# Pooled attention and a gated two-layer block in one kernel: batch 1's k pooled on GpSimd, its v on VectorE, and four accumulators for the first down product

## The chip, the core and the metric

The kernel runs on one core of a Trainium2 chip. The core has TensorE (matrix products, written to PSUM), VectorE, ScalarE (activation functions), GpSimd and SyncE, each with an instruction queue of its own that runs in order, and 16 DMA engines that move data between HBM and SBUF. Engines wait for each other and for transfers by semaphores. The metric is the device time of one execution in microseconds (us).

Names in the profile: PE is TensorE's matmul, PEld its weight load, DVE is VectorE, ACT ScalarE, POOL GpSimd, SP SyncE. `L321` is line 321 of the kernel before. A program's tile names stand without their numbers: `bank` for bank0 to bank2.

## The reference

```python
def _attn_ref(q, k, v) -> np.ndarray:
    B, H, S, D = q.shape
    pool = 8
    Sp = S // pool
    scale = 1.0 / np.sqrt(D)
    k_p = k.reshape(B, H, Sp, pool, D).mean(axis=3)
    v_p = v.reshape(B, H, Sp, pool, D).mean(axis=3)
    scores = scale * np.matmul(q, k_p.transpose(0, 1, 3, 2))
    scores = scores - np.max(scores, axis=-1, keepdims=True)
    attn = np.exp(scores)
    attn = attn / (np.sum(attn, axis=-1, keepdims=True) + 1e-09)
    return np.matmul(attn, v_p).astype(np.float32)

def _moe_ref(x, w_in, w_out) -> np.ndarray:
    h = x @ w_in
    g = h * np.cos(h)
    return (g @ w_out).astype(np.float32)
```

q, k and v are 8 x 8 x 576 x 64 (batch, heads, rows, width), so Sp is 72; `w_in` is 512 x 2048 and `w_out` 2048 x 512. The attention's output, with its heads side by side, is x: 8 batches of 576 rows are 4608 tokens of width 512.

## The kernel before

**Tiles.** The 4608 tokens are worked in nine tiles of 512 (`NT`, loop variable `t`). Batches have 576 rows, so a tile's attention comes from two batches: while tile `t` is worked, the last 64 rows of batch `t` (`REST`) and the first 512 rows of batch `t+1` (variable `b`) go through the attention. The instructions of each engine run in the order in which the program emits them.

**A tile's two phases.** The up phase has eight steps `fp` of eight matmuls each (`up_mm`, L321): x transposed (`xT`) times `w_in`, into `banks[fp % 3]`. There are three `banks`, each a pair of PSUM banks, and two single `obanks`. `up_g` takes the cosine on ScalarE (L328) and multiplies on VectorE (L331) into `g_sb`. For tiles after the first, the first half of steps 0 and 1 is emitted ahead of the rest. The down phase has 64 matmuls (`down_mm`, L334): for each of four groups of 128 tokens (`ms`) 16 chunks of the inner dimension (`fc`), accumulated in `obanks[ms % 2]`, then copied out by VectorE and stored by SyncE (`down_out`, L340, L344).

**Fillers.** The list `fill` of pairs (n, function) puts the attention's TensorE work between the down matmuls: a function is emitted ahead of down matmul n. `scores` (L214, with the exponential on ScalarE at L221) and `values` (L244: matmuls, then logarithm and exponential on ScalarE, L250 and L251, then two multiplies on VectorE into `xT`, L255) work a unit of 256 rows by four heads, or `REST` by all eight heads. Both write one of `banks`, and it is free for the next user when the exponential, or for values the last multiply, has read it. Units of batch 1 are `us[0]` to `us[3]`: heads 0 to 3 and then 4 to 7, two blocks of rows each.

**Batches 0 and 1 before, and the others.** The loads of q, k and v go through GpSimd's DMA queue, which converts fp32 to bf16; the weights go through it as well. For batches 0 and 1 k and v are laid out over 128 rows (`load_even`) and pooled on TensorE with a matrix of ones (`groups`): `pool_k_mm`, 72 matmuls (L160), and `pool_v_mm`, 18 (L168), with copies out of PSUM by `put_kk` (L132) and L170. For batch 1, k's pooling is emitted at step 4 of tile 0's up phase, the 18 transposes of q (L195, copies L196) at steps 5 and 6, and v's pooling ahead of down matmul 8. From batch 2 on k and v are loaded with eight rows side by side over 72 partitions (`load_kv`, L103) and pooled on GpSimd by three rounds of adds (`pool_add`, L142, L145, then L148 for k, written twice, or L151 for v); k is transposed by a DMA on SyncE (`k_transpose`), q by another.

**Loads around the change.** The order on GpSimd's queue is: q, k, q, v of batch 0; `w_in` blocks 0 to 2; k of batch 1; half of its q; `w_in` block 3; the other half; `w_out` block 0; v of batch 1; three memsets; `w_out` blocks 1 to 3; and, emitted after tile 0, k, q and v of batch 2 and the pooling of batch 2 (the second part of v's in tile 1). The staging tiles `kv_st` have two buffers, handed out in turn: in before one holds k and v of batch 0 and the other those of batch 1, then each one k or one v.

**Tile 0's down matmuls** go in an order of their own, since the last `w_out` blocks arrive late: for each half of the tokens (two `ms`) through the four `w_out` blocks, so block c is first used by matmul 8c, and each half's two accumulators are the two `obanks`.

Of the kernel before, what the change touches and what calls it, by code (L numbers as in the profile page):

```python
# [14 lines left out]
POOL = 8  # L15
# [4 lines left out]
def kernel(  # L20
# [65 lines left out]
    def kv_tile():  # L86
        return kvst.tile([128, 2 * H * POOL * D], BF16, name="kv_st", tag="kv_st")
# [11 lines left out]

    def load_kv(b, which, src):  # L100

        st = kv_tile()[:Sp].rearrange("p (i h t d) -> p i h t d", i=2, h=H, t=POOL)
        nc.gpsimd.dma_start(out=st[:, 0].rearrange("p h t d -> p h (t d)"),  # L103
                            in_=src[b].rearrange("h (p t) d -> p h (t d)", t=POOL))
        staged[which, b] = st

# [26 lines left out]

    def pool_add(b, which, part=None):

        st = staged[which, b]
        x = st[:, 0]
        s = st[:, 1].rearrange("p h t d -> p (h t d)").bitcast(FP32).rearrange(
            "p (h t d) -> p h t d", h=H, t=POOL // 2)
        add = nc.gpsimd.tensor_tensor  # L140
        if part != 1:
            add(out=s, in0=x[:, :, 0:4, :], in1=x[:, :, 4:8, :], op=ADD)  # L142
        if part == 0:
            return
        add(out=s[:, :, 0:2, :], in0=s[:, :, 0:2, :], in1=s[:, :, 2:4, :], op=ADD)  # L145
        if which == "k":
            for slot in range(2):
                add(out=kp2[b % 2][:Sp, :, slot, :], in0=s[:, :, 0, :], in1=s[:, :, 1, :], op=ADD)  # L148
        else:
            s = s.rearrange("p (j a) t d -> p j a t d", a=2)  # L150
            add(out=v_part(b), in0=s[..., 0, :], in1=s[..., 1, :], op=ADD)  # L151

# [20 lines left out]
    def k_transpose(b):  # L173
        nc.sync.dma_start_transpose(out=kk[b % 2], in_=kp2[b % 2].rearrange("p h s d -> p (h s d)"))


    QB = KCH * ROW // 2
# [218 lines left out]

    kv_even_tiles(1)
    q_tile(1)
    for cg in range(3):
        load_w_in(cg)  # L400
    load_even(staged["k", 1], 1, k)
    load_even(staged["q", 1], 1, q, 0, 2)
    load_w_in(3)
    load_even(staged["q", 1], 1, q, 2, 4)
    load_w_out(0)
    load_even(staged["v", 1], 1, v)
    nc.gpsimd.memset(vz[1], float(POOL))
    for i in range(2):
        nc.gpsimd.memset(kp2[i], 0.0)
    for cg in range(1, 4):  # L410
        load_w_out(cg)

# [43 lines left out]
    for t in range(NT):  # L456
# [5 lines left out]
        for fp in range(FFCH // 2):  # L462
            up_mm(t, fp, 2 if fp < 2 else 0)
            between = ()
            if t == 0:
                if fp == 4:
                    puts = pool_k_mm(1, obanks[0], 0, 2), pool_k_mm(1, obanks[1], 2, 4)
                elif fp in (5, 6):
                    g0 = 9 * (fp - 5)
                    puts = q_transpose_mm(1, obanks[0], g0, g0 + 5), q_transpose_mm(1, obanks[1], g0 + 5, g0 + 9)  # L470
                if fp in (4, 5, 6):
                    puts[0](vec)
                    between = ((puts[1], act),)
            up_g(t, fp, between)
            if 0 < t and b < B:
                if fp == 0:
                    q_transpose(b)
                elif fp == 2:
                    k_transpose(b)
                    if t == 1:  # L480
                        load_next(b)
                        pool_add(b, "v", 1)
                        load_kv(b + 1, "v", v)
        mms = [(ms, fc) for ms in range(4) for fc in range(FFCH)]
        if t == 0:
            mms = [(ms, fc) for hm in range(2) for cg in range(4) for ms in range(2 * hm, 2 * hm + 2)
                   for fc in range(4 * cg, 4 * cg + 4)]


        def S_(n, bank):  # L490
            return lambda: scores(b, us[n], banks[bank])

        later = []

        def V_(n, bank, wait=None):
            return lambda: values(b, us[n], banks[bank], wait)

# [4 lines left out]
        if t == 0:  # L502
            fill[1:] = [(2, S_(0, 0)), (8, lambda: pool_v_mm(1, banks[1])), (8, lambda: values(t, REST, banks[2])),
                        (11, S_(1, 0)), (13, V_(0, 1)), (18, S_(2, 2)), (21, V_(1, 0, later)), (26, S_(3, 1)),
                        (32, lambda: later.pop()()), (32, V_(2, 2)), (40, V_(3, 0))]
        elif b < B:
            us = BY_TOKENS

            def scores_of(*parts):

                def go():
                    for f in scores_mm, scores_exp:
                        for b_, u, bank in parts:
                            f(b_, u, banks[bank])
                return go

            def rows_of(i, blk, bank):
# [4 lines left out]
                    (42, rows_of(1, 0, 0)), (44, rows_of(1, 1, 1)), (47, lambda: values(t, REST, banks[2]))]  # L522
        fi = 0
        if t == NT - 1:
            mms = mms[:-FFCH]
        for n, (ms, fc) in enumerate(mms):
            while fi < len(fill) and fill[fi][0] <= n:
                fill[fi][1]()
                fi += 1
            down_mm(obanks[ms % 2], ms, fc)  # L530
            if fc == FFCH - 1:
                down_out(t, ms, obanks[ms % 2])
        if t < B:
# [36 lines left out]
```

## Time and profile before

| | |
|---|---|
| median of 3 runs | 297.28 us (296.84 to 297.56) |
| the profiled execution's own time | 296.36 us |
| its span, first to last instruction | 294.6 us |
| tile 0: first up matmul, first down matmul | 17.2 us, 33.6 us |
| first up matmul of tiles 1, 2 and 3 | 52.96, 83.32, 113.67 us |

The span is what the profile's rows cover; the execution's own time has 1.8 us more around it. The profile's table of busy times says how much of the span each engine worked, the slices say when, and the chain that ended last says which work the end waited for, step by step backwards.

Between 10 and 47 us the DMA engines move 206 GB/s on average. What lands when, from the DMA issues one by one (issue plus time to landing):

| load | issued, us | landed, us |
|---|---|---|
| w_in block 2 | 6.64 | 20.94 |
| k of batch 1 | 7.37 | 23.77 |
| first half of q of batch 1 | 8.10 | 25.2 |
| w_in block 3 | 9.32 | 27.8 |
| w_out block 0 | 13.56 | 31.7 |
| v of batch 1 | 16.10 | 34.5 |
| w_out blocks 1, 2, 3 | 19.51, 21.20, 24.03 | 37.1, 39.9, 42.3 |
| k, q, v of batch 2 | 25.83, 28.07, 37.52 | 46.2, 48.9, 54.2 |

### The profile page before, as it was taken

How to read it: one execution, taken by the hardware profiler on the slowest of the kernel's cores; microseconds unless marked ns; L12 is line 12 of the kernel's file. 1: busy time of each engine (PE TensorE's matmuls, PEld its weight loads, DVE VectorE, ACT ScalarE, POOL GpSimd, SP SyncE). 2: the span in 40 equal slices, each digit the busy share in tenths (PEclk: the TensorE clock that was granted, in tenths of full speed). 3: DMA queues.
4: the chain of work that ended last, by engine and by line, in shares of the span. 5: the costliest groups of instructions: out<-in, count | busy, mean ns of one | idle time of the engine just before them, and what ended most of it. 6: DMA issues, size and time to landing. Idle time of an engine off the chain costs nothing.

```text
span 294.6 us, 4775 instructions
## 1 busy us (share of the span) xinstructions
PE 287.7 (98%) x1912; PEld 140.2 (48%) x1912; DVE 158.8 (54%) x212; ACT 162.1 (55%) x182; POOL 130.5 (44%) x93
## 2 busy tenths in 40 slices
PE   8899999999999999999999999999999999999995
PEld 3545544444544454445444544455445544444444
DVE  5458647466347643764375456645574557416612
ACT  3886898365446734673468337743675456506500
POOL 8563017968973696349833983399000000000000
PEclk9999999999999999999999999999999999999999
DMA  7999999659966975698469747994603320131033
GB/s 151 204 207 206 207 205 207 137 95 178 157 155 93 167 128 131 112 170 149 108 122 169 147 92 139 162 148 103 142 2 71 81 64 0 36 73 36 0 71 73
DMA packets 57222, 36.07 MB, mean 122 GB/s; under 512 B 35185, under 2 KB 52465, under 8 KB 57201
## 3 DMA queue, kind: packets, MB, share of 16 engines
q0 software_dynamic: 19744, 18.07, 39.4%
q1 hardware_dynamic: 37216, 17.57, 28.6%
q8 instruction: 15, 0.25, 0.4%
q10 hardware_dynamic: 240, 0.13, 0.2%
q14 instruction: 7, 0.05, 0.0%
HBM read 36.70 MB, written 9.44 MB: 157 GB/s over the span
## 4 chain that ended last, share of the span: by engine, by line
PE 93%; DVE 1%; issue 0%; DVEq 0%
PE bank L321 42%; PE obank L334 42%; PE bank L214 3%; PE bank L301 2%; PE bank L244 1%; PE bank L352 1%; PE obank L160 0%; PE bank L168 0%; PE obank L283 0%; PE obank L195 0%; DVE xT L285 0%; DVE vz L170 0%; DVE o_sb L340 0%; DVEq L285 0%
## 5 line engine op out<-in xcount | busy, mean ns | idle before, releaser
L334 PE MATMUL obank<-w_out_sb,g_sb 128*128 128x512 bf16 x560 | 131.4, 379 | 0.0
L321 PE MATMUL bank<-xT,w_in_sb 128*128 128x512 bf16 x576 | 126.6, 379 | 0.0
L328 ACT ACTIVATE cos<-bank,half_pi 128x1024 f32<-128x1024 f32 x72 | 79.3, 1114 | 70.4 <-PE bank L321 70.4
L331 DVE TENSOR_TENSOR g_sb<-bank,cos 128x1024 bf16<-128x1024 f32 x72 | 87.3, 1223 | 51.6 <-ACT cos L328 51.6
L321 PEld LDWEIGHTS <-w_in_sb 128*128 128x128 bf16 x576 | 56.1, 98 | 67.6 <-issue 1.6
L334 PEld LDWEIGHTS <-g_sb 128*128 128x128 bf16 x560 | 51.6, 98 | 56.6 <-issue 2.0
L142 POOL TENSOR_TENSOR kv_st<-kv_st 72x2048 f32<-72x2048 bf16 x12 | 48.7, 4058 | 30.4 <-DMA kv_st<-in_k_dram 30.4
L340 DVE COPY o_sb<-obank 128x512 f32<-128x512 f32 x35 | 24.2, 692 | 46.9 <-PE obank L334 46.7
L221 ACT ACTIVATE ex<-bank 72x1024 bf16<-72x1024 f32 (+1 forms) x40 | 35.0, 929 | 21.2 <-PE bank L214 21.1
L145 POOL TENSOR_TENSOR kv_st<-kv_st 72x1024 f32<-72x1024 f32 x12 | 28.2, 2348 | 0.9
L250 ACT ACTIVATE lnc<-bank 64x256 f32<-64x256 f32 (+1 forms) x24 | 10.8, 449 | 17.9 <-PE bank L244 17.7
L255 DVE TENSOR_TENSOR xT<-bank,inv 64x256 bf16<-64x256 f32 (+1 forms) x24 | 12.3, 511 | 10.8 <-ACT inv L251 10.6
L304 DVE TENSOR_TENSOR x_r<-bank,inv_r 128x512 bf16<-128x512 f32 x24 | 16.6, 691 | 0.8
L148 POOL TENSOR_TENSOR kp<-kv_st 72x512 bf16<-72x512 f32 x12 | 14.9, 1265 | 0.5
L214 PE MATMUL bank<-qT,kk 64*72 64x256 bf16 (+1 forms) x192 | 11.9, 250 | 0.4 <-DVE qT L196 0.4
L214 PEld LDWEIGHTS <-kk 64*72 64x72 bf16 x192 | 7.9, 110 | 8.7 <-issue 7.4
L309 ACT ACT_TABLE_LOAD x9 | 11.5, 1283 | 0.9 <-PEq L554 0.7
L312 ACT ACT_TABLE_LOAD x9 | 11.5, 1283 | 0.2
L301 PEld LDWEIGHTS <-ex 72*128 72x128 bf16 x192 | 8.9, 97 | 5.0
L452 POOL COPY gate<-kk 1x1 bf16<-1x1 bf16 x5 | 0.9, 180 | 22.7 <-DMA kk<-kp 22.7
L302 DVE RECIPROCAL inv_r<-bank 128x8 f32<-128x8 f32 x24 | 4.8, 202 | 10.7 <-PE bank L301 10.7
L301 PE MATMUL bank<-vz,ex 72*128 72x65 bf16 x192 | 9.8, 192 | 0.0
(59 smaller groups left out, 113.9 us busy)
## 6 DMA issues: line engine op xcount, KB each, us to landing
out_dram<-o_sb SPq DMA_DIRECT2D x70, 128.0 KB, 2.4
kv_st<-in_v_dram POOLq DMA_DIRECT2D x8, 576.0 KB, 12.9
kv_st<-in_k_dram POOLq DMA_DIRECT2D x7, 576.0 KB, 7.9
q_b<-in_q_dram POOLq DMA_DIRECT2D x6, 576.0 KB, 10.0
w_in_sb<-in_moe_w_in_dram POOLq DMA_DIRECT2D x4, 512.0 KB, 13.4
w_out_sb<-in_moe_w_out_dram POOLq DMA_DIRECT2D x4, 512.0 KB, 18.2
q_b<-in_q_dram POOLq DMA_DIRECT2D x4, 288.0 KB, 12.2
g_sb<-in_k_dram SPq DMA_DIRECT2D x1, 576.0 KB, 3.6
```

The costliest lines, as they stand in the source:

```text
L142: add(out=s, in0=x[:, :, 0:4, :], in1=x[:, :, 4:8, :], op=ADD)
L145: add(out=s[:, :, 0:2, :], in0=s[:, :, 0:2, :], in1=s[:, :, 2:4, :], op=ADD)
L148: add(out=kp2[b % 2][:Sp, :, slot, :], in0=s[:, :, 0, :], in1=s[:, :, 1, :], op=ADD)
L214: nc.tensor.matmul(pair[:Sp, bank, c:c + n].rearrange("p (g n) -> p g n", n=64), lhsT=kk[b % 2][half[r], h0 + i, 0:Sp], rhs=att["qT", b][h ...
L221: nc.scalar.activation(out=ex[:, 0:nh * n].rearrange("p (a n) -> p a n", a=2), in_=pair[:Sp, :, 0:nh * n // 2], func=ACTF.Exp, scale=scale ...
L301: nc.tensor.matmul(out[:, pj, hp * (D + 1):(hp + 1) * (D + 1)], lhsT=ex[:, c:c + 128], rhs=v1)
L304: nc.vector.tensor_mul(out=x, in0=vals, in1=inv.unsqueeze(3).to_broadcast([128, KCH, 2, D]))
L321: nc.tensor.matmul(h[:, j, :], lhsT=w_in_sb[fc // 4][:, ki, (fc % 4) * 128:(fc % 4 + 1) * 128], rhs=xT[:, ki, t * TILE:(t + 1) * TILE], st ...
L328: nc.scalar.activation(out=cos, in_=h, func=ACTF.Sin, bias=half_pi[:, :1])
L331: nc.vector.tensor_mul(out=g_sb[:, 2 * fp:2 * fp + 2, :], in0=h, in1=cos)
L334: nc.tensor.matmul(o, lhsT=g_sb[:, fc, ms * 128:(ms + 1) * 128], rhs=w_out_sb[fc // 4][:, fc % 4, :], start=(fc == 0), stop=(fc == FFCH - 1))
L340: nc.vector.tensor_copy(out=o[:, 0:n], in_=ps)
```

## The change

For batch 1 alone, k and v are loaded as for later batches, over 72 partitions. k is pooled by GpSimd's adds (8.9 us of busy time for a k in the profile before), emitted between the issues of the last two `w_out` blocks, and the pooled k is transposed by eight TensorE transposes into one `obank`, with one copy out (new function `k_transpose_mm`). v is loaded in two halves of four heads and pooled by the same three rounds of adds, on VectorE, for each half. Its staging buffer is the one that batch 0's k and v had. The loads go in this order after `w_in` block 2: k, `w_in` block 3, half of q, `w_out` block 0, the other half of q, half of v, the memsets, `w_out` block 1, the other half of v, `w_out` block 2, [pooling of k], `w_out` block 3.

In tile 0's up phase only one group of nine q transposes is left, at step 6; the other nine, the k transposes and v's adds are emitted ahead of down matmuls 5, 6 and 7. Tile 0's down matmuls go through `w_out` block by block for all four groups of tokens, so block c is first used by matmul 16c, and there are four accumulators: the two halves of `banks[2]` and the two `obanks`. The four outputs are thus finished by matmuls 51, 55, 59 and 63. The scores of batch 1 are emitted in pairs of units, and the fillers use `banks[0]` and `banks[1]` alone; the last unit of values stands ahead of down matmul 52, on `banks[0]` (before: matmul 40).

```diff
@@ -97,12 +97,12 @@
     def q_tile(b):
         staged["q", b] = qst.tile([128, KCH, ROW, D], BF16, name="q_b", tag="q_b")
 
-    def load_kv(b, which, src):
-
-        st = kv_tile()[:Sp].rearrange("p (i h t d) -> p i h t d", i=2, h=H, t=POOL)
-        nc.gpsimd.dma_start(out=st[:, 0].rearrange("p h t d -> p h (t d)"),
-                            in_=src[b].rearrange("h (p t) d -> p h (t d)", t=POOL))
-        staged[which, b] = st
+    def load_kv(b, which, src, h0=0, h1=H):
+
+        if h0 == 0:
+            staged[which, b] = kv_tile()[:Sp].rearrange("p (i h t d) -> p i h t d", i=2, h=H, t=POOL)
+        nc.gpsimd.dma_start(out=staged[which, b][:, 0, h0:h1].rearrange("p h t d -> p h (t d)"),
+                            in_=src[b, h0:h1].rearrange("h (p t) d -> p h (t d)", t=POOL))
 
     def load_q(b):
         q_tile(b)
@@ -131,13 +131,12 @@
             for r in range(2):
                 copy(out=dst[half[r], pj0:pj1, a, 0:Sp], in_=ps[half[a]])
 
-    def pool_add(b, which, part=None):
+    def pool_add(b, which, part=None, add=nc.gpsimd.tensor_tensor, h0=0, h1=H):
 
         st = staged[which, b]
-        x = st[:, 0]
+        x = st[:, 0, h0:h1]
         s = st[:, 1].rearrange("p h t d -> p (h t d)").bitcast(FP32).rearrange(
-            "p (h t d) -> p h t d", h=H, t=POOL // 2)
-        add = nc.gpsimd.tensor_tensor
+            "p (h t d) -> p h t d", h=H, t=POOL // 2)[:, h0:h1]
         if part != 1:
             add(out=s, in0=x[:, :, 0:4, :], in1=x[:, :, 4:8, :], op=ADD)
         if part == 0:
@@ -148,7 +147,7 @@
                 add(out=kp2[b % 2][:Sp, :, slot, :], in0=s[:, :, 0, :], in1=s[:, :, 1, :], op=ADD)
         else:
             s = s.rearrange("p (j a) t d -> p j a t d", a=2)
-            add(out=v_part(b), in0=s[..., 0, :], in1=s[..., 1, :], op=ADD)
+            add(out=v_part(b)[:, h0 // 2:h1 // 2], in0=s[..., 0, :], in1=s[..., 1, :], op=ADD)
 
     def pool_k_mm(b, bank, pj0, pj1):
 
@@ -173,6 +172,14 @@
     def k_transpose(b):
         nc.sync.dma_start_transpose(out=kk[b % 2], in_=kp2[b % 2].rearrange("p h s d -> p (h s d)"))
 
+
+    def k_transpose_mm(b, bank):
+
+        ps = bank.bitcast(BF16)[:, 0:H * Sp].rearrange("p (h n) -> p h n", n=Sp)
+        for h in range(H):
+            nc.tensor.matmul(ps[:, h, :], kp2[b % 2][:Sp, h].rearrange("p s d -> p (s d)"), identity[:Sp, :Sp],
+                             is_transpose=True)
+        nc.vector.tensor_copy(out=kk[b % 2][:, :, 0:Sp], in_=ps)
 
     QB = KCH * ROW // 2
 
@@ -394,21 +401,23 @@
     half_pi = consts.tile([128, 1], FP32, name="half_pi")
     nc.vector.memset(half_pi, math.pi / 2.0)
 
-    kv_even_tiles(1)
     q_tile(1)
     for cg in range(3):
         load_w_in(cg)
-    load_even(staged["k", 1], 1, k)
+    load_kv(1, "k", k)
+    load_w_in(3)
     load_even(staged["q", 1], 1, q, 0, 2)
-    load_w_in(3)
+    load_w_out(0)
     load_even(staged["q", 1], 1, q, 2, 4)
-    load_w_out(0)
-    load_even(staged["v", 1], 1, v)
-    nc.gpsimd.memset(vz[1], float(POOL))
+    load_kv(1, "v", v, 0, 4)
     for i in range(2):
         nc.gpsimd.memset(kp2[i], 0.0)
-    for cg in range(1, 4):
-        load_w_out(cg)
+    nc.gpsimd.memset(vz[1], float(POOL))
+    load_w_out(1)
+    load_kv(1, "v", v, 4, 8)
+    load_w_out(2)
+    pool_add(1, "k")
+    load_w_out(3)
 
     def warm_up(n, bank):
 
@@ -463,12 +472,8 @@
             up_mm(t, fp, 2 if fp < 2 else 0)
             between = ()
             if t == 0:
-                if fp == 4:
-                    puts = pool_k_mm(1, obanks[0], 0, 2), pool_k_mm(1, obanks[1], 2, 4)
-                elif fp in (5, 6):
-                    g0 = 9 * (fp - 5)
-                    puts = q_transpose_mm(1, obanks[0], g0, g0 + 5), q_transpose_mm(1, obanks[1], g0 + 5, g0 + 9)
-                if fp in (4, 5, 6):
+                if fp == 6:
+                    puts = q_transpose_mm(1, obanks[0], 0, 5), q_transpose_mm(1, obanks[1], 5, 9)
                     puts[0](vec)
                     between = ((puts[1], act),)
             up_g(t, fp, between)
@@ -483,36 +488,39 @@
                         load_kv(b + 1, "v", v)
         mms = [(ms, fc) for ms in range(4) for fc in range(FFCH)]
         if t == 0:
-            mms = [(ms, fc) for hm in range(2) for cg in range(4) for ms in range(2 * hm, 2 * hm + 2)
-                   for fc in range(4 * cg, 4 * cg + 4)]
-
-
-        def S_(n, bank):
-            return lambda: scores(b, us[n], banks[bank])
-
-        later = []
-
-        def V_(n, bank, wait=None):
-            return lambda: values(b, us[n], banks[bank], wait)
+            mms = [(ms, fc) for cg in range(4) for ms in range(4) for fc in range(4 * cg, 4 * cg + 4)]
+
+
+        def scores_of(*parts):
+
+            def go():
+                for f in scores_mm, scores_exp:
+                    for b_, u, bank in parts:
+                        f(b_, u, banks[bank])
+            return go
+
+        def late_q():
+            puts = q_transpose_mm(1, banks[0][:, 0, :], 9, 14), q_transpose_mm(1, banks[0][:, 1, :], 14, 18)
+            puts[0](vec)
+            puts[1](act)
+
+        def pool_v():
+            for h0 in (0, 4):
+                pool_add(1, "v", add=nc.vector.tensor_tensor, h0=h0, h1=h0 + 4)
+
+        def V_(n, bank):
+            return lambda: values(b, us[n], banks[bank])
 
         fill = []
         if t < B:
             exp_tables()
             fill = [(1, lambda: scores(t, REST, banks[2])), (16, lambda: values(t, REST, banks[1]))]
         if t == 0:
-            fill[1:] = [(2, S_(0, 0)), (8, lambda: pool_v_mm(1, banks[1])), (8, lambda: values(t, REST, banks[2])),
-                        (11, S_(1, 0)), (13, V_(0, 1)), (18, S_(2, 2)), (21, V_(1, 0, later)), (26, S_(3, 1)),
-                        (32, lambda: later.pop()()), (32, V_(2, 2)), (40, V_(3, 0))]
+            fill = [(5, late_q), (6, lambda: k_transpose_mm(1, obanks[1])), (7, pool_v), (14, scores_of((1, us[0], 0), (1, us[1], 1))),
+                    (20, lambda: scores(0, REST, banks[0])), (25, scores_of((1, us[2], 0), (1, us[3], 1))),
+                    (30, V_(0, 0)), (35, V_(1, 1)), (41, lambda: values(0, REST, banks[0])), (46, V_(2, 1)), (52, V_(3, 0))]
         elif b < B:
             us = BY_TOKENS
-
-            def scores_of(*parts):
-
-                def go():
-                    for f in scores_mm, scores_exp:
-                        for b_, u, bank in parts:
-                            f(b_, u, banks[bank])
-                return go
 
             def rows_of(i, blk, bank):
                 return lambda: values_rows(b, us[2 * i:2 * i + 2], blk, banks[bank])
@@ -521,15 +529,18 @@
                     (29, scores_of((b, us[2], 0), (b, us[3], 1), (t, REST, 2))),
                     (42, rows_of(1, 0, 0)), (44, rows_of(1, 1, 1)), (47, lambda: values(t, REST, banks[2]))]
         fi = 0
+        acc = [obanks[ms % 2] for ms in range(4)]
+        if t == 0:
+            acc = [banks[2][:, 0, :], banks[2][:, 1, :], obanks[0], obanks[1]]
         if t == NT - 1:
             mms = mms[:-FFCH]
         for n, (ms, fc) in enumerate(mms):
             while fi < len(fill) and fill[fi][0] <= n:
                 fill[fi][1]()
                 fi += 1
-            down_mm(obanks[ms % 2], ms, fc)
+            down_mm(acc[ms], ms, fc)
             if fc == FFCH - 1:
-                down_out(t, ms, obanks[ms % 2])
+                down_out(t, ms, acc[ms])
         if t < B:
             sin_tables()
         if b + 1 < B:
```

## The prediction

> **What bounds the kernel now.** I read the page first: busy table, slices, chain that ended last.
>
> ```profile
> span 294.6 us, 4775 instructions
> PE 287.7 (98%) x1912; PEld 140.2 (48%) x1912; DVE 158.8 (54%) x212; ACT 162.1 (55%) x182; POOL 130.5 (44%) x93
> PEclk9999999999999999999999999999999999999999
> PE 93%; DVE 1%; issue 0%; DVEq 0%
> ```
>
> TensorE is the bound, at full granted clock throughout. The edit touches the stretch from the first up matmul to the first up matmul of tile 1, so next I read the chain of waits for that window, whose pieces show what each filler costs TensorE:
>
> ```profile
> 17.21 8.79 PE bank L321 x40
> 26.01 1.29 PE obank L160 x72
> ...
> 29.13 0.50 PE obank L195 x9
> ...
> 36.12 1.10 PE bank L168 x18
> ...
> 39.09 0.44 PE bank L244 x4
> 39.53 1.08 PE obank L334 x5
> ...
> 47.78 5.18 PE obank L334 x24
> 52.96 0.65 PE bank L321 x3
> ```
>
> (Start, duration, what.) A down matmul costs 5.18/24 = 0.216 us. Tile 1's first matmul starts at 52.96, and from there TensorE runs without a hole (tile 2 starts at 83.32, tile 3 at 113.67, 30.35 us each). So the change is worth what it moves 52.96 by, and the profiled run moves one for one.
>
> Last, GpSimd's timeline and the DMA issues, asked for one by one (last column: us from issue to landing; the issues are at 6.64, 7.37, 24.03 and 25.83):
>
> ```profile
> 24.03 0.74 POOL L117 DMA_DIRECT2D w_out_sb<-in_moe_w_out_dram  x1 [2.08 <-DMA kv_st<-in_k_dram]
> 46.28 4.06 POOL L142 TENSOR_TENSOR kv_st<-kv_st 72x2048 f32<-72x2048 bf16 x1 [7.92 <-DMA kv_st<-in_k_dram]
> 50.42 2.35 POOL L145 TENSOR_TENSOR kv_st<-kv_st 72x1024 f32<-72x1024 f32 x1
> 52.85 2.49 POOL L148 TENSOR_TENSOR kp<-kv_st 72x512 bf16<-72x512 f32 x2
> w_in_sb<-in_moe_w_in_dram POOLq DMA_DIRECT2D x1, 512.0 KB, 14.3
> kv_st<-in_k_dram POOLq DMA_DIRECT2D x1, 576.0 KB, 16.4
> w_out_sb<-in_moe_w_out_dram POOLq DMA_DIRECT2D x1, 512.0 KB, 18.3
> kv_st<-in_k_dram POOLq DMA_DIRECT2D x1, 576.0 KB, 20.4
> ```
>
> Three readings. GpSimd pools one k in 55.34 - 46.28 = 9.06 us. The issue at 24.03 is the 16th of its queue and waited for the landing of the 8th; every late issue there follows the one eight before it. And the same 576 KB of k take longer in the 72-row layout: batch 1's k (128 rows) landed at 23.77, 2.83 us after the third w_in (20.94); batch 2's k (72 rows) at 46.23, 3.90 us after the last w_out (42.33).
>
> **TensorE work removed and added.** Gone: 72 pooling matmuls of k (1.29) and 18 of v (1.10) = 2.39 us. Added: 8 transposes of pooled k, between 0.26 (eight score matmuls of 64 columns) and 0.44 (8/9 of the 0.50 for nine q transposes); I take 0.44, the same operation. Nine of the 18 q transposes move into the down phase, at no change. Score groups of four become pairs of eight: five switches from score matmuls back, each making the next run about 0.1 longer (1.40 for six instead of 1.30), become three, which saves 0.2. TensorE is thus relieved of some 2.1 us, if nothing waits.
>
> **Up phase.** fp 4 ends at 26.01 as before; fp 5 at 27.74, fp 6 at 29.47, nine transposes 29.97, fp 7 at 31.70, where the down matmuls start (33.59 before). Loads, spaced as the trace has them (2.5 us a 512 KB weight block, 1.4 a q half, 3.90 a 72-row k, half of it for half a v): k 24.84, last w_in 27.4 (wanted 27.74), q half 28.8 (29.47), first w_out 31.3 (31.70), q half 32.75 (32.78), v half 34.7, w_out 37.2, v half 39.1, w_out 41.7. Each is just in time, and a slip of up to 1.5 us would vanish in the next wait. With k as early as before, all come about 1 us sooner.
>
> **The wait for k.** Behind five down matmuls (1.08), nine transposes (0.50) and one more down matmul (0.22) TensorE reaches the k transposes at 33.50. They need GpSimd. Its queue holds the issue of the third w_out ahead of the pooling; that is the 16th and waits for the 8th, which is k itself: 24.84 + 0.26 + 0.74 for the issue + 0.06 = 25.90, plus 9.06 = 34.96, and about 0.1 to TensorE: 35.05. A new wait of 1.55 us, and everything on TensorE is queued behind it. Bounds: 0.5 us, were k to land at 23.77; nothing, were GpSimd done before 33.50, which its row excludes unless k lands before 23.3. I take 24.84, by the row of the same layout. Also behind the pooling on GpSimd: the issue of the last w_out (24.03 before, about 35 now; wanted by matmul 48 at about 49, landing about 44), then batch 2's k and q, then its v, whose buffer VectorE's pooling must first free (about 41.5). Their pooled use is in tile 1 at 67.6, and batch 2's k still lands about when it did, behind the same bytes: no cost. On SyncE the eight stores of tile 0 come after 50 instead of from 44.85, ahead of the same two transposes, whose results are wanted at 67.6: no cost.
>
> **v on VectorE.** Six adds, two halves of 1024, 512 and 256 elements a row. Nearest VectorE rows: 1.22 (L331, 1024), 0.69 (L340, 512), 0.42 (L255, 256), about 2.4 a half with gaps. The upper bound is half of GpSimd's times for the same adds, 2.03 + 1.17 + 0.63 = 3.83. I take 2.4. The k copy out of PSUM ends at 35.95 (0.45 by L196); first half to 38.4; second from its landing at 39.1 to 41.5. VectorE stands still meanwhile, but nothing behind it is due before 44.9. The first values matmul comes at 42.37 (below), so 0.9 us of cover hides the adds.
>
> The Trainium skill speaks against these adds: SBUF — State Buffer, "Who interferes with whom", has a VectorE instruction with two SBUF inputs and a GpSimd instruction that reads SBUF exclude each other for whole instructions. No row of before has that pair. By it the sum changes only if the adds meet a pooling. GpSimd's next pooling stands behind the load of batch 2's v, and that behind VectorE's last add, so by the order of the queues they never meet.
>
> **The tail.** From 35.05: transposes 0.44, eight matmuls 1.73, so matmul 14 is at 37.23. Then a score pair 0.66, six matmuls 1.30, rest scores 0.36, five 1.08, a pair 0.66, five 1.08: the first values at 37.23 + 5.14 = 42.37. From here, counted from 0 at that point. A values unit is 0.44 on TensorE, then ScalarE 1.20 + 0.63 and VectorE 1.39 (L250, L251, L255), and its bank is free only then. ScalarE is done with the second pair's exponentials at 0.63. Unit 0: ScalarE 0.65 to 2.50, VectorE to 3.92. Unit 1 (1.52 to 1.96 on TensorE): to 4.35 and 5.77. The rest unit is due at 3.26 on unit 0's bank: waits to 3.98 (0.72), is off VectorE at 6.65. Unit 2 is due at 5.36 on unit 1's bank: waits to 5.83 (0.47); ScalarE to 8.22, VectorE to 9.64. Unit 3 at 7.57 to 8.01; ScalarE to 10.07; on VectorE an output copy of 0.69 goes ahead, so it ends at 11.72. The twelve matmuls left end at 10.61, and tile 1 starts on the same bank 0: waits to 11.78 (1.17). In before, 24 matmuls (5.18) followed the last unit and hid this.
>
> Sum: 42.37 + 11.78 = 54.15 against 52.96, **1.19 us slower**. Checked by parts: waits 1.55 + 0.72 + 0.47 + 1.17 = 3.91, less 2.1 of work, less about 0.6 of small stalls that before had (0.17 at 47.17 among them), is 1.2. The profiled run took 296.36 (span 294.6), the median is 297.28; the shift goes on the median: 298.5.
>
> **Rivals.**
> 1. k lands as early as before, since its layout costs less where no store runs: transposes at 33.98, tile 1 at 53.08, +0.12 us, **297.4**. For: batch 2's k landed with other traffic near. Against: while only such k loads run (65.5 to 67) the DMA moves 157 GB/s, against 205 in 14 to 18; 0.59 MB at 157 is 3.76 us.
> 2. Faster: the bank waits of the tail don't form, because matmuls start on the half bank whose multiply is done and the chain from values to free bank is shorter. It decides from a chain under about 2.8 us instead of 3.5; then 0.72 + 0.47 + 1.17 = 2.36 go, -1.17 us, **296.1**. For: the multiply is two instructions, one for each half. Against: at 47.17 the last unit of before started just after both halves were done (45.72 + 1.39), not after one.
> 3. Much slower: VectorE's adds run at GpSimd's pace. 35.95 + 7.7 = 43.65, first values 1.3 us later, +2.5, **299.8**. It decides from adds of 2.9 us a half. Against: L385, two fp32 inputs from SBUF, 648 elements in 0.83 us, is no slower than VectorE's other rows.
>
> **How the numbers follow.** Forecast 0.60, rival 1 0.20, rival 2 0.13, rival 3 0.07. 0.2% is 0.6 us, about what a measurement can tell from no change. The forecast's own range is 297.9 to 299.2, with 0.06 of its chance under +0.6. Slower: 0.54 + 0.07, with a little of rival 1: 0.62. Same: 0.06 and most of rival 1: 0.24. Faster: 0.14. The range reaches to a part of rivals 2 and 3: 296.6 to 299.5.
>
> **What would show it.** k's load landing at 24.8; GpSimd's pooling ending near 35.0; a hole on TensorE of 1.5 us ahead of the k transposes with GpSimd as its releaser; VectorE's adds at 1.2, 0.7 and 0.4; holes of 0.7 and 0.5 before matmuls 41 and 46, and of 1.2 at tile 1's first matmul, released by VectorE's L255; tile 1 at 54.1. A k landing below 24 makes it wrong by a microsecond, absent holes in the tail by two. A later tile that isn't 30.35 us would break the one-for-one shift.

## The result, and the profile after

The changed kernel takes 299.66 us (median of 6 runs, 299.07 to 301.05) where the kernel before, on the same chip, takes 296.79: a ratio of 1.0104, 95% interval 1.0074 to 1.0134. It is slower, as forecast, by 2.9 us where 1.2 were forecast, and 0.16 us beyond the end of the range. The profiled run took 299.77 us.

Most lines of the changed kernel are 7 higher than before: the up matmuls are L328, the down matmuls L341, values L251 with L257, L258 and the multiply L262, the output copy L347. The three rounds of adds are one lower, L141, L144 and L147 or L150, and the k transposes are L180.

The page of the changed kernel, the lines that answer to those of before:

```profile
span 297.8 us, 4579 instructions
PE 283.2 (95%) x1797; PEld 137.9 (46%) x1830; DVE 161.7 (54%) x214; ACT 161.3 (54%) x178; POOL 140.4 (47%) x98
PE 82%; DMA 6%; POOL 5%; ACT 2%; issue 2%; DVE 1%; POOLq 0%; ACTq 0%
```

TensorE's busy time fell by 4.5 us (33 of its 1830 matmul records are missing from this trace, so a part of that is not real) and the span grew by 3.2. The chain that ended last no longer stays on TensorE: it runs through a transfer (6%), GpSimd (5%) and ScalarE. Its pieces, in order of time (start, duration, what):

```profile
7.36 18.01 DMA kv_st<-in_k_dram
...
25.65 0.75 POOL w_out_sb L117
...
26.43 4.09 POOL kv_st L141
...
30.59 2.37 POOL kv_st L144
...
35.57 0.43 PE obank L180 x8
...
52.70 0.70 DVE o_sb L347
...
53.45 1.02 PE bank L341 x4
54.47 1.51 PE obank L341 x7
...
56.03 2.11 PE bank L328 x9
```

Up to 35.57 this is the chain that the prediction worked out: the load of k, the issue of a w_out block, the pooling, the transposes. Tile 1 starts at 56.03 instead of 52.96, 3.07 us later, and later tiles follow at 86.55 and 116.90. The forecast was 54.15. The holes in TensorE's timeline show where the rest is (in brackets the idle time before the row, and who ended it):

```profile
27.94 1.90 PE L328 MATMUL bank<-xT,w_in_sb 128*128 128x512 bf16 x7 [0.62 <-DMA w_in_sb<-in_moe_w_in_dram]
35.57 0.43 PE L180 MATMUL obank<-identity,kp 72*128 72x72 bf16 x8 [1.32 <-POOL kp L147]
46.80 0.41 PE L251 MATMUL bank<-ex,vz 72*128 72x64 bf16 x8 [0.68 <-DVE xT L262]
48.69 0.61 PE L251 MATMUL bank<-ex,vz 72*128 72x256 bf16 x4 [0.40 <-DVE xT L262]
53.45 1.02 PE L341 MATMUL bank<-w_out_sb,g_sb 128*128 128x512 bf16 x4 [2.40 <-DVE o_sb L347]
```

The second, third and fourth row were forecast (1.55, 0.72, 0.47). The last was not. It is the longest: down matmul 52, the first one behind the last values unit, waits for an output copy. VectorE's timeline at that place:

```profile
51.28 1.39 DVE L262 TENSOR_TENSOR xT<-bank,inv 64x512 bf16<-64x512 f32 x2 [1.75 <-ACT inv L258]
52.70 0.69 DVE L347 COPY o_sb<-bank 128x512 f32<-128x512 f32 x1
53.42 1.39 DVE L262 TENSOR_TENSOR xT<-bank,inv 64x512 bf16<-64x512 f32 x2
```

The copy empties group 0's accumulator, the first half of `banks[2]`. Matmul 52 writes group 1's accumulator, the second half of the same tile. The copy could have gone when matmul 51 ended (about 50.5), but stands on VectorE behind the multiply of values unit 2, which waits for ScalarE until 51.28.

The six runs fall into two kinds: four at 299.07 to 299.77 with a mean granted clock (the share of full speed that TensorE's clock was granted) of 1.0, and two at 300.91 and 301.05 with 0.994. That difference is followed up below. Three runs of the later comparisons lie so far out, with clocks of 0.982 to 0.987 (one of e4_keven at 304.40 us, one of c4_spaced at 299.73, one of the kernel before at 301.85), that the ratios leave them out, while the medians hold them.

### The profile page after: what moved, and what is told of

It is laid out like the page before. It is cut to its first block, busy times and chain, and to the rows that moved or that the text cites. A ratio compares the mean times of both kernels' runs of the same rounds, so it can differ in the third digit from the quotient of the medians.

```text
span 297.8 us, 4579 instructions
## 1 busy us (share of the span) xinstructions
PE 283.2 (95%) x1797; PEld 137.9 (46%) x1830; DVE 161.7 (54%) x214; ACT 161.3 (54%) x178; POOL 140.4 (47%) x98
## 4 chain that ended last, share of the span: by engine, by line
PE 82%; DMA 6%; POOL 5%; ACT 2%; issue 2%; DVE 1%; POOLq 0%; ACTq 0%
PE bank L328 37%; PE obank L341 37%; DMA kv_st<-in_k_dram 6%; PE bank L221 3%; PE bank L308 2%; POOL kv_st L141 1%; ACT lnc L257 1%; PE bank L359 1%; PE bank L341 1%; POOL kv_st L144 1%; PE bank L251 1%; POOL w_in_sb L112 1%; ACT ex L228 1%; ACT inv L258 1%; POOL q_b L84 1%
## 5 line engine op out<-in xcount | busy, mean ns | idle before, releaser
L328 PE MATMUL bank<-xT,w_in_sb 128*128 128x512 bf16 x564 | 125.8, 379 | 1.3 <-DMA w_in_sb<-in_moe_w_in_dram 0.6
L341 PE MATMUL obank<-w_out_sb,g_sb 128*128 128x512 bf16 x510 | 120.8, 379 | 1.2 <-issue 0.6
L328 PEld LDWEIGHTS <-w_in_sb 128*128 128x128 bf16 x576 | 56.1, 98 | 69.0 <-issue 1.6
L341 PEld LDWEIGHTS <-g_sb 128*128 128x128 bf16 x560 | 51.5, 98 | 59.0 <-issue 4.6
L141 POOL TENSOR_TENSOR kv_st<-kv_st 72x2048 f32<-72x2048 bf16 x13 | 52.8, 4061 | 27.0 <-DMA kv_st<-in_k_dram 27.0
L347 DVE COPY o_sb<-obank 128x512 f32<-128x512 f32 x33 | 22.8, 692 | 44.5 <-PE obank L341 44.2
L144 POOL TENSOR_TENSOR kv_st<-kv_st 72x1024 f32<-72x1024 f32 x13 | 30.5, 2348 | 1.0
L257 ACT ACTIVATE lnc<-bank 64x256 f32<-64x256 f32 (+1 forms) x24 | 10.8, 449 | 18.2 <-PE bank L251 17.8
L262 DVE TENSOR_TENSOR xT<-bank,inv 64x256 bf16<-64x256 f32 (+1 forms) x24 | 12.3, 511 | 13.2 <-ACT inv L258 13.0
L147 POOL TENSOR_TENSOR kp<-kv_st 72x512 bf16<-72x512 f32 x14 | 17.4, 1266 | 0.6
L341 PE MATMUL bank<-w_out_sb,g_sb 128*128 128x512 bf16 x31 | 8.3, 379 | 2.5 <-DVE o_sb L347 2.4
```

Source lines behind the costliest of these rows:

```text
L328: nc.tensor.matmul(h[:, j, :], lhsT=w_in_sb[fc // 4][:, ki, (fc % 4) * 128:(fc % 4 + 1) * 128], rhs=xT[:, ki, t * TILE:(t + 1) * TILE], st ...
L341: nc.tensor.matmul(o, lhsT=g_sb[:, fc, ms * 128:(ms + 1) * 128], rhs=w_out_sb[fc // 4][:, fc % 4, :], start=(fc == 0), stop=(fc == FFCH - 1))
L347: nc.vector.tensor_copy(out=o[:, 0:n], in_=ps)
```

## The experiments

All kernels below are the changed kernel with the edit shown. Times are medians; each ratio is to the kernel before, run on the same chip. The columns on the right are from the profiled run: the start of the first values unit and of tile 1's first up matmul, in us. The 52.96 of the kernel before is read from its chain of waits; its row in the timeline, from which the others are read, starts at 52.80.

| kernel | us | ratio, 95% interval | first values | tile 1 |
|---|---|---|---|---|
| before | 296.79 | | | 52.96 |
| changed | 299.66 | 1.0104 (1.0074 to 1.0134) | 42.71 | 56.03 |
| e1_outs | 298.07 | 1.0045 (1.0026 to 1.0064) | 42.74 | 54.65 |
| e8_swap | 299.04, one run | | 42.92 | 55.37 |
| e2_issue | 299.21 | 1.0087 (1.0053 to 1.0120) | 41.57 | 56.31 |
| e3_ktlate | 300.25 | 1.0117 (1.0076 to 1.0158) | 44.28 | 57.61 |
| e4_keven | 299.88 | 1.0082 (1.0059 to 1.0106) | 41.29 | 56.30 |
| e7_keven_outs | 299.98 | 1.0106 (1.0085 to 1.0127) | 42.03 | 53.94 |
| e6_split | 297.79 | 1.0041 (1.0027 to 1.0055) | 42.21 | 54.11 |
| e5_restlast | 297.47 | 1.0030 (1.0019 to 1.0041) | 43.19 | 54.15 |
| c2_all | 296.20 | 0.9984 (0.9973 to 0.9994) | 41.81 | 52.90 |
| c3_split | 296.01 | 0.9971 (0.9958 to 0.9984) | 40.62 | 51.71 |
| c4_spaced | 295.72 | 0.9965 (0.9951 to 0.9978) | 40.46 | 51.56 |
| e9_longhole | 302.09 | 1.0179 (1.0155 to 1.0202) | | 59.38 |

### The unexpected hole: e1_outs and e8_swap

```diff
-            if fc == FFCH - 1:
-                down_out(t, ms, acc[ms])
+            if fc == FFCH - 1 and (t > 0 or ms > 0):
+                for m in (0, 1) if t == 0 and ms == 1 else (ms,):
+                    down_out(t, m, acc[m])
```

> The changed kernel with one edit: tile 0's first output copy is emitted after the second group's last matmul (55) instead of after matmul 51. Theory A (the two accumulators in the halves of banks[2] count as one tile, so down matmul 52 waits for the copy of the first output, which on VectorE stands behind unit 2's multiply): the hole of 2.40 us ahead of matmul 52 goes, the twelve matmuls end at 50.9 + 2.6 = 53.5, tile 1 then waits for the last multiply on bank 0, which ends near 54.6: first up matmul of tile 1 at 54.7 instead of 56.03, 1.3 us faster, 298.3. Rival B (matmul 52 waits for the multiply of unit 2 itself, or for the stored outputs): the hole stays at 1.7 us or more, and tile 1 starts at 55.4 or later.

The hole ahead of matmul 52 is gone, and tile 1 starts at 54.65 with a wait of 0.98 for the last multiply on bank 0. Theory A forecast 54.7 and 298.3; 298.07 was measured. So 1.4 us of the loss at tile 1 is this one wait, net of the wait on bank 0 that it had been hiding. What is left of the loss against the kernel before is 298.07 - 296.66 = 1.41 us.

e8_swap asks whether it is the tile that joins the two accumulators. The copy stays where the change put it, and only the accumulators change places:

```diff
-            acc = [banks[2][:, 0, :], banks[2][:, 1, :], obanks[0], obanks[1]]
+            acc = [banks[2][:, 0, :], obanks[0], banks[2][:, 1, :], obanks[1]]
```

> The changed kernel with one edit: the four accumulators in another order, so that banks[2] holds groups 0 and 2 and the single banks groups 1 and 3; the first output is copied where it was. Theory A (the wait goes with the tile: a matmul into one half of banks[2] waits for the copy out of the other half): matmuls 52 to 55 run at once, and the hole stands ahead of matmul 56, which writes banks[2] again; the copy ends when it did, near 53.4, so the hole is about 1.5 us. Rival B (the matmul after the last values unit waits for VectorE whatever it writes): the hole stays ahead of matmul 52 at 2.4 us.

TensorE's timeline of e8_swap around the last values unit:

```profile
50.64 0.60 PE L251 MATMUL bank<-ex,vz 72*128 72x256 bf16 x4
51.08 1.03 PE L341 MATMUL obank<-w_out_sb,g_sb 128*128 128x512 bf16 x4
53.65 1.02 PE L341 MATMUL bank<-w_out_sb,g_sb 128*128 128x512 bf16 x4 [1.54 <-DVE o_sb L347]
```

Matmuls 52 to 55 now write an `obank` and run at once (51.08); the hole stands ahead of matmul 56, which writes the other half of `banks[2]`, and is 1.54 us where 1.5 was forecast. The wait goes with the tile, not with the place.

### The wait for k: e2_issue, e3_ktlate, e4_keven, e7_keven_outs

e2_issue takes the issue of w_out block 2 out of the chain:

```diff
-    load_w_out(2)
     pool_add(1, "k")
+    load_w_out(2)
     load_w_out(3)
```

> The changed kernel with one edit: the issue of w_out block 2 moves behind the pooling of k on GpSimd's queue. Theory A (the wait for k is on TensorE's path one for one): the pooling starts 0.78 us earlier (25.65 instead of 26.43), the k transposes at 34.8 instead of 35.57, and tile 1 at 55.25 instead of 56.03; w_out block 2 lands near 40.7 as before, since the queue of bytes ahead of it is the same. Rival B (the tail is set by the landing of v's second half, 38.2, and VectorE's adds): the hole ahead of the k transposes shrinks to 0.5 us, but tile 1 stays within 0.2 us of 56.03.

The k transposes start at 34.28 behind a hole of 0.31, 1.29 us earlier than in the changed kernel, and the first values unit and matmul 52 come 1.14 us earlier (52.31 for 53.45): 0.78 for the issue, and 0.3 because k landed at 25.07 instead of 25.37 in this run. That is one for one, as theory A has it. Tile 1 did not follow, for a reason that the expectation did not have. The windows of e2_issue (stretch, length, busy time and count of PE, PEld, DVE, ACT and POOL, granted clock of TensorE, DMA share, GB/s):

```profile
50.00:51.50 1.50, 0.00 (x0) 0.00 (x0) 1.34 (x2) 1.42 (x4) 1.50 (x1) 1.00 0.91 151
51.50:52.50 1.00, 0.19 (x1) 0.10 (x1) 0.94 (x3) 0.98 (x2) 0.96 (x1) 0.64 0.77 137
52.50:55.00 2.50, 2.50 (x7) 0.91 (x6) 1.86 (x3) 0.80 (x1) 2.38 (x2) 0.50 0.65 141
55.00:56.00 1.00, 1.00 (x6) 0.39 (x4) 0.35 (x1) 0.00 (x0) 1.00 (x1) 0.90 0.00 0
```

Inside the hole the granted clock drops to a half, and stays there until about 55.2: seven matmuls in 2.5 us instead of eleven or twelve. Two of e2_issue's four runs have a mean clock of 0.993 or 0.994 (299.92 and 300.27 us), the two at 0.999 and 1.0 took 298.15 and 298.51, about 1.1 below the changed kernel's undisturbed four. e9_longhole comes back to this.

e3_ktlate puts the k transposes behind five more down matmuls:

```diff
-(6, lambda: k_transpose_mm(1, obanks[1])), (7, pool_v),
+(11, lambda: k_transpose_mm(1, banks[1][:, 0, :])), (11, pool_v),
```

> The changed kernel with one edit: the k transposes go ahead of down matmul 11 instead of 6, into a half of banks[1], so that five more down matmuls run before TensorE waits. Theory A: the hole of 1.3 us shrinks to 0.3, the first score pair comes at 36.7 instead of 37.7, tile 1 at 55.0 instead of 56.03 (1.0 us faster). Rival B (tail set by v): the hole moves to the first values unit, which waits for VectorE's adds (done at 41.2 in the changed kernel), and tile 1 stays within 0.3 us.

Inconclusive by itself. In its profiled run batch 0's v landed at 14.84 (12.84 for the changed kernel), which left a hole of 2.07 us there, and the clock was at a half from 15.7 to 22.5. TensorE came to the k transposes so late (38.23) that no wait was left to be seen. Its one run at a clock of 1.0 took 298.55. In c2_all, which holds the same edit, no wait for k is left.

e4_keven undoes the k part: k over 128 rows and pooled on TensorE at step 4, as before.

```diff
-    load_kv(1, "k", k)
+    staged["k", 1] = even_part(kv_tile(), 0)
+    load_even(staged["k", 1], 1, k)
...
-    pool_add(1, "k")
...
+                if fp == 4:
+                    puts = pool_k_mm(1, obanks[0], 0, 2), pool_k_mm(1, obanks[1], 2, 4)
...
-(6, lambda: k_transpose_mm(1, obanks[1])), (7, pool_v),
+(7, pool_v),
```

> The changed kernel with its k part undone: batch 1's k loaded over 128 rows and pooled on TensorE at step 4 of the up phase, as in the kernel before; all else as changed. TensorE has 1.29 - 0.43 = 0.86 us more work. Theory A (the removed work is given back as the wait for k, and the 72-row load delays the loads behind it): no holes of 0.6 ahead of step 6 and 1.3 ahead of the k transposes, first score pair at 36.1 instead of 37.7, tile 1 at 54.4 instead of 56.0, 298.0. Rival B (only TensorE's work counts): 0.9 us slower than the changed kernel, 300.5.

With 0.86 us more to do, TensorE reaches the first values unit 1.42 us earlier (41.29) and matmul 52 at 52.03 instead of 53.45; neither of the two early holes is there. Rival B falls. Then the clock dropped again, this time just behind the hole ahead of matmul 52 (at a half from 52.4 to 55.8), and tile 1 started at 56.30. e7_keven_outs is the same with e1_outs' edit:

> e1_outs with the k part undone (as e4_keven): batch 1's k pooled on TensorE, 0.86 us more TensorE work than e1_outs. Theory A (the work taken from TensorE is given back as the wait for k): the first values unit at 41.3 instead of 42.74, tile 1 at 53.2 instead of 54.65, about 296.9. Rival B (only TensorE's work counts): 0.9 us slower than e1_outs. Without the hole of 2.4 us ahead of matmul 52 the granted clock stays at 0.997 or more in every run, where e2_issue, e3_ktlate and e4_keven had runs at 0.98 to 0.994.

Tile 1 starts at 53.94, 0.7 us before e1_outs, where 1.45 were forecast. In e7_keven_outs the first values unit is 24.43 us behind the first up matmul (17.60), exactly as in e4_keven (16.86 and 41.29), so half of the forecast gain went into a later start of the up phase in this run, which e1_outs, held up by k until 35.60, would not have felt: its own up phase began at 17.77, 1.0 later than the changed kernel's, and its k transposes came only 0.03 later. The clock is 0.998 or more in all four runs, as forecast. The total, though, is 1.9 us above e1_outs. In the profiled runs tile 2 starts 1.44 us later than in e1_outs (86.45 for 85.01), and this is why:

```profile
86.45 14.02 PE L328 MATMUL bank<-xT,w_in_sb 128*128 128x512 bf16 x62 [1.99 <-DMA xT<-x_r]
```

Tile 2's first up matmul waits 1.99 us for transposes by DMA on SyncE's queue, which landed 6.1 us after the first of them was issued at 80.30. e4_keven's profiled run has no such wait. Three of e7_keven_outs' four runs are at 299.8 to 300.3 and one at 298.63, so the wait may come and go; only one of the four was profiled. The loads for batch 3 were under way at the time; that they held the transpose up was not tried. That the k part costs more than it saves is thus shown up to tile 1, and not for the whole kernel.

### The 72-row load: e6_split

e1_outs with k loaded in two transfers:

```diff
-    load_kv(1, "k", k)
+    staged["k", 1] = kv_tile()[:Sp].rearrange("p (i h t d) -> p i h t d", i=2, h=H, t=POOL)
+    for p0, p1 in ((0, 64), (64, Sp)):
+        nc.gpsimd.dma_start(out=staged["k", 1][p0:p1, 0].rearrange("p h t d -> p h (t d)"),
+                            in_=k[1].rearrange("h (p t) d -> p h (t d)", t=POOL)[p0:p1])
```

> e1_outs with batch 1's k loaded as two transfers, 64 rows and 8 rows (same bytes, one more issue of 0.8 us on GpSimd). Theory A (a transfer of 72 rows uses 12 of the 16 DMA engines, one of 64 rows uses all): k lands 3.1 us after the third w_in block instead of 3.8, pooling and k transposes 0.7 us earlier (34.9 instead of 35.6), tile 1 at 54.0 instead of 54.65. Rival B (the 72-row layout is slow for another reason, such as its reads from HBM): k lands 3.8 us after, or later by the extra issue, no gain.

In the changed kernel k lands at 25.37, 3.8 us after the third w_in block (21.55), which repeats the 3.9 of batch 2's k. Split, its two parts land at 24.0 and 24.9, the later 3.3 us after that block (21.6). The k transposes come at 35.07 instead of 35.60 and tile 1 at 54.11 instead of 54.65, which is 0.54 of theory A's 0.7 us. A part of this is chance: in e1_outs k landed 3.6 us after that block, and the block itself 0.2 later. All profiled runs together show the direction more surely. From that block's landing to the last of k it takes 3.4 to 4.3 us in the eight with one transfer of 72 rows, 2.7 to 3.3 us in the three with the split one (e6_split, c3_split, c4_spaced), and 2.8 to 2.9 us in the three with 128 rows (before, e4_keven, e7_keven_outs). The medians (297.79 and 298.07) have intervals that overlap.

The Trainium skill (DMA: Bandwidth & Descriptors, "Why a DMA increments its semaphore by 16 and not by 1") has a transfer run on the largest number of engines, up to 16, that divides the slowest dimension of both its sides, which is 12 for 72 rows, with an exception for some plain copies on GpSimd's queue. The 157 GB/s against 205 of the profile before (0.77, where 12/16 is 0.75) and this experiment agree with the 12; no view here counts the engines themselves.

### The tail: e5_restlast

e1_outs with the rest's unit last:

```diff
-(35, V_(1, 1)), (41, lambda: values(0, REST, banks[0])), (46, V_(2, 1)), (52, V_(3, 0))]
+(35, V_(1, 1)), (41, V_(2, 0)), (46, V_(3, 1)), (52, lambda: values(0, REST, banks[0]))]
```

> e1_outs with one more edit: the rest's values unit goes last (ahead of matmul 52) and units 2 and 3 move up to 41 and 46. Theory A (what is left of the tail is the chain matmuls, logarithm, exponential, multiply, which holds a bank for 4.0 us after a unit's start; the rest's chain is 0.8 us shorter than a full unit's): from the first values unit to tile 1 takes 10.9 us instead of 11.9, tile 1 at 53.7 instead of 54.65, about 297.1 against 298.1 of e1_outs; no wait of tile 1 on bank 0 is left. Rival B (the tail's length is TensorE's work plus waits on loads): no change against e1_outs.

From the first values unit to tile 1 it takes 54.15 - 43.19 = 10.96 us, against 54.65 - 42.74 = 11.91 in e1_outs; 10.9 was forecast. TensorE no longer waits ahead of tile 1. So the chain through ScalarE and VectorE behind the last unit, and the bank it holds meanwhile, is what still held tile 1 up in e1_outs.

### All mends together: c2_all, c3_split, c4_spaced

c2_all has the edits of e1_outs, e2_issue, e3_ktlate and e5_restlast.

> All four mends at once on the changed kernel: both output copies after matmul 55, w_out block 2 issued behind the pooling, k transposes ahead of matmul 11, the rest's values last. Theory A (four separate waits, each worth what the single edits showed): no wait for k, score pair at 36.1, first values unit at 41.1, tile 1 at 52.0, 0.9 us before that of the kernel before: 295.8 against 296.7. Rival B (v's second half, landed near 38.2, and the adds behind it set the first values unit): it cannot start before 41.3 and waits, tile 1 at 52.6 or later, no faster than before.

c2_all is a little faster than the kernel before: 296.20 us, 0.9984 (0.9973 to 0.9994). There is no wait for k (transposes at 35.18), but tile 1 starts at 52.90, not 52.0. New waits took a part of it:

```profile
27.90 1.90 PE L328 MATMUL bank<-xT,w_in_sb 128*128 128x512 bf16 x7 [0.27 <-DMA w_in_sb<-in_moe_w_in_dram]
...
33.37 0.68 PE L202 MATMUL bank<-identity,q_b 128*128 128x128 bf16 x9 [0.17 <-DMA q_b<-in_q_dram]
...
37.76 1.02 PE L341 MATMUL bank<-w_out_sb,g_sb 128*128 128x512 bf16 x4 [0.42 <-DMA w_out_sb<-in_moe_w_out_dram]
```

All three wait for loads that stand behind the 72-row k on the same queue. c3_split adds e6_split's edit:

> c2_all with batch 1's k loaded as 64 rows and 8 rows. Theory A (in c2_all the loads behind the 72-row k set the pace: waits of 0.27 at step 6, 0.17 for q, 0.42 for w_out block 1): these waits go, tile 1 at 52.3 instead of 52.9, 295.6 against 296.6 of the kernel before. Rival B (the second half of v and the adds set the first values unit, done at 41.3 in c2_all): tile 1 within 0.2 us of c2_all.

These waits go: the first values unit is at 40.62, tile 1 at 51.71, 296.01 us, 0.9971 (0.9958 to 0.9984). c4_spaced moves the last three values units apart and the copies to the end:

```diff
-(41, V_(2, 0)), (46, V_(3, 1)), (52, lambda: values(0, REST, banks[0]))]
+(43, V_(2, 0)), (49, V_(3, 1)), (55, lambda: values(0, REST, banks[0]))]
```

> c3_split with the last three values units further apart (43, 49, 55 instead of 41, 46, 52) and all four output copies after matmul 63. Theory A (what is left are waits of 0.7, 0.2 and 0.2 for banks in the values chain, with twelve matmuls behind the last unit): from the first values unit to tile 1 takes 10.75 us instead of 11.1, tile 1 0.3 us earlier than in c3_split, 295.3. Rival B: the rest's multiply now ends after the last matmul and tile 1 waits for it, no gain over c3_split.

```profile
44.55 0.61 PE L251 MATMUL bank<-ex,vz 72*128 72x256 bf16 x4 [0.24 <-DVE xT L262]
...
48.59 0.41 PE L251 MATMUL bank<-ex,vz 72*128 72x64 bf16 x8 [0.24 <-DVE xT L262]
...
51.56 6.68 PE L328 MATMUL bank<-xT,w_in_sb 128*128 128x512 bf16 x30 [0.84 <-DVE xT L262]
```

Rival B came true: what the bank waits gave up came back as a wait of 0.84 ahead of tile 1, and the stretch takes 11.10 us, as in c3_split (11.09). 295.72 us is the lowest median of the study, 0.9965 (0.9951 to 0.9978); it can't be told from c3_split's.

### The clock: e9_longhole

```diff
             if fc == FFCH - 1:
+                if t == 0 and ms == 0:
+                    for i in range(2):
+                        nc.vector.tensor_copy(out=spare, in_=acc[0])
                 down_out(t, ms, acc[ms])
```

> The changed kernel with two more copies of the first accumulator on VectorE (0.69 us each, into a spare tile) ahead of the first output copy, so that the hole ahead of matmul 52 grows from 2.40 to 3.8 us. Theory A (a hole of this length on TensorE is what halves the granted clock for some 3.4 us, and at 2.4 us it depends on the moment): nearly every run has a mean clock of 0.994 or less, and the time is 1.4 us for the longer hole and 1.2 to 1.7 us for the half clock above the undisturbed runs of the changed kernel (299.4): 302 to 302.5. Rival B (the lower clock comes from elsewhere): about a third of the runs have it, as for the changed kernel, and the others are at 300.8.

The hole ahead of matmul 52 is 3.73 us, the mean clock of the five runs 0.989, 0.994, 0.994, 0.989 and 0.994, and the median 302.09, as theory A has it. The windows of its profiled run, with the columns of e2_issue's:

```profile
52.00:53.00 1.00, 0.00 (x0) 0.00 (x0) 0.94 (x3) 0.95 (x3) 1.00 (x1) 1.00 0.19 31
53.00:54.00 1.00, 0.00 (x0) 0.00 (x0) 1.00 (x2) 0.98 (x1) 0.92 (x2) 0.51 0.00 0
54.00:55.00 1.00, 0.69 (x2) 0.25 (x2) 0.95 (x3) 0.00 (x0) 1.00 (x2) 0.50 0.00 0
...
58.00:59.00 1.00, 1.00 (x3) 0.34 (x3) 0.61 (x1) 0.00 (x0) 1.00 (x1) 0.50 0.85 197
59.00:60.00 1.00, 0.78 (x3) 0.37 (x3) 0.38 (x1) 0.00 (x0) 1.00 (x1) 0.58 0.53 123
```

The half clock begins at 53.0, inside the hole and 2.4 us after TensorE went idle (50.6), and in this run lasts until 59.8.

## Why the prediction was right in its sign and wrong in its size

**The step that failed** is in the tail: "Unit 3 at 7.57 to 8.01 ... The twelve matmuls left end at 10.61, and tile 1 starts on the same bank 0: waits to 11.78 (1.17)." The first four of those twelve were taken to depend on nothing. They write the second half of `banks[2]`, and had to wait 2.40 us for the copy out of its first half (e1_outs, e8_swap). The last term was right in its turn: with the copy out of the way, tile 1 does wait 0.98 us on bank 0 (e1_outs); in the changed kernel the longer hole covered it. I counted the banks that the fillers share one by one and didn't ask the same of the accumulators. The sign was not luck: with this one wait taken away (e1_outs) the loss is 1.41 us, where 1.19 was forecast for a kernel without it.

**The account of 56.03 against 54.15.** The k transposes came 0.52 later (35.57 for 35.05), since k landed at 25.37 and not 24.84. From there to the first values unit 0.18 was won back (7.14 us for 7.32). The tail took 13.32 us instead of 11.78: 0.16 because the values chain held a bank 4.04 us and not 3.92; 2.40 - 1.17 = 1.23 for the hole; 0.15 at its edges. 0.52 - 0.18 + 1.54 = 1.88.

**The wait for k** was right in mechanism and price, and is shown by e2_issue: 1.32 for 1.55. It is smaller since TensorE was ready later, at 34.25 instead of 33.50: a wait of 0.62 for w_in block 3, forecast as just missed, came ahead of it and, as the prediction had it, cost nothing more. The term that was too small is k's landing: its spacing was right (3.9 forecast, 3.8 measured), but the block ahead of it landed at 21.55 instead of 20.94. Behind the same loads that block landed between 20.7 and 22.1 in the profiled runs, so this 0.6 us is chance and not the change.

**v on VectorE** was right: adds of 1.21, 0.69 and 0.42, done at 41.2 (41.5 forecast), the first values unit at 42.71. The adds met no pooling on GpSimd, so the exclusion that was weighed there stays untested.

**What was left out**: the clock. Two runs of the changed kernel in six lost another 1.5 us to it. The median of all six is 299.66, that of the other four 299.43.

**The rivals.** Rival 1 (k lands as early as before) is refuted by the landing at 25.37. Rival 2 (no bank waits in the tail) by the rows at 46.80 and 48.69. Rival 3 named the right size for a wrong reason: VectorE's adds ran at VectorE's pace.

**One for one.** The shift is 3.07 us at tile 1, 3.2 at tile 2 (86.55 for 83.32) and in the span, 2.9 in the medians: what is lost in tile 0 is not made up.

## What to carry to other kernels

When an accumulator moves, list for each matmul that opens or continues it what last read its tile, the other half of the tile too, and what stands ahead of that reader on its own engine. Work taken off the busiest engine is worth its time only if the engine that takes it over is done before the busiest one asks: here 1.29 us of pooling on TensorE became 9.1 us on GpSimd behind a load that landed later, and a wait of 1.32. With the issue, the copy, the transposes and the order of the last units moved and the load split, the same division of work is faster than the kernel before by 1.0 us (c4_spaced).

## What the runs showed of the hardware that was not expected

TensorE's granted clock fell to a half in or just behind idle stretches of little more than two microseconds. It stayed there for 3.4 us (e2_issue, 51.8 to 55.2; e4_keven, 52.4 to 55.8, from 0.4 us behind the hole on) or for twice as long (e9_longhole, 53.0 to 59.8; e3_ktlate, 15.7 to 22.5, from 0.9 us behind an early hole of 2.07 us on). With the hole of 2.40 us some executions have a mean clock of 0.994 or less: two of six of the changed kernel, two of four of e2_issue, three of four of e3_ktlate (the profiled one through its early hole alone), two of four of e4_keven. With the hole of 3.73 us all five have it. Of the kernels without that hole, none of the 46 runs of e1_outs, e5_restlast, e6_split, e7_keven_outs, c2_all and c3_split is below 0.997. One of twelve of c4_spaced (0.987) and one of 61 of the kernel before (0.983) are, and neither was profiled, so what lowered the clock in those two stays open. The Trainium skill (TensorE: Matmul & The Clock Gate, "What's actually happening") has the clock throttled after an idle window of about 3.4 us. Here the drop came 2.4 us after TensorE went idle in e9_longhole and 1.9 us after in e2_issue (49.9 to 51.8), so a shorter idle stretch was enough.

A transfer of 72 rows took 3.8 us, from the landing ahead of it to its own, where the same bytes over 128 rows took 2.8 (k of batch 1, changed kernel and before). The transfers behind it were late by about that difference (w_in block 3 landed 6.3 us after block 2 in the changed kernel and 5.4 in e4_keven, where k has 128 rows), so that weights which TensorE wanted in the up phase became the next wait (0.62 ahead of step 6).
